# Four low weight parts made by ScalarE and an adding transfer, and a regrouped start, in a fused linear-attention and two-layer kernel

## The chip, the cores and the metric

One NeuronCore of a Trainium2 chip runs the whole program. The metric is device time in microseconds (us); the time before is the median of three runs. Engines are called PE (TensorE matmuls), PEld (its weight loads), DVE (VectorE), ACT (ScalarE), POOL (GpSimd) and SP (SyncE, which here issues nearly all transfers).

## The reference

The first stage is a linear attention with a complex decay: batch 4, 8 heads, 768 steps, head width 48. The two later stages are dense layers over 3072 tokens, with a width of 384 and a hidden width of 2048.

```
mag = sqrt(a_re*a_re + a_im*a_im)
scale = minimum(mag, 0.999) / (mag + 1e-06)
S_re, S_im = (a*scale) * (S_re + i S_im) + k v^T        (one step of 768)
y[t] = q[t] S_re
h = x @ w_in ;  x = (h - tanh(h)) @ w_out               (first layer)
h = x @ w_in ;  x = max(h, 0)**2 @ w_out                (second layer)
```

## The kernel before, in words

The 768 steps are cut into six chunks of 128, and with four batches this makes 24 units, numbered n = 4c + b for chunk c and batch b. Units 0 to 3 are chunk 0 and are computed ahead of everything else. Later units are spread over the steps of the first layer by a plan. The first layer works in blocks: one block is one slice m (128 of the 2048 hidden columns, m = 0 to 15) for 512 tokens. A block computes h with `g1`, then t, gh and gl (`act_parts`), and adds to three banks of `acc` with `g2`. Every factor is split into a rounded high part and a low part, so each product takes three matmuls: wh with xh, wh with xl, wl with xh.

The weights arrive as raw 64-bit words in a tile `st`, loaded by SP (`conv_load`, L205). `conv_do` (L214) rebuilds 32-bit floats in a tile `cv` with three DVE instructions (one TENSOR_SCALAR, two SCALAR_TENSOR_TENSOR). `cv` has two buffers, so slice m takes the buffer of slice m-2, and its first instruction has to wait until that buffer is no longer read. `conv_split` (L270) then calls `split_w` (L276): ACT rounds `cv` into `wh`, and DVE subtracts, `wl = cv - wh`. This happens for slices 0 to 15 of the first layer one after another, between 10 and 133 us.

The start is written out by hand in `START` (L32): a number and a name stand for one part of one unit (`0sq` is `a1` of unit 0, `0ln` is `a2`, `0ph` is `a3`, `0pc` is `a6l`), J is one third of a weight conversion. Between `<` and `>` the instructions of ACT and of DVE are chained, each engine issuing in the listed order; outside it a list scheduler orders each engine's queue at build time. For units 0 to 3, `a1` (L460) squares re and im into the two halves A and B of a tile `ab` (ACT for units 0 and 2, DVE for 1 and 3), and then one DVE instruction writes B = max(A, const) + B. `a2` (L472) is on ACT: logarithm of A in place, logarithm of B in place, X = exp(-B/2) into half G of a tile `fg`, exp(-A/2) in place. `a3` (L486) is on DVE: B = min(B, const) - X, then im = im * A. Half F of `fg` is first written later, in `a7` (L544). Two masks are made on DVE at L131 (`tri`) and L135 (`maskt`) from a mask that POOL writes at L112 to L122; these two are outside the chain. PE reads `maskt` first in the sums `pu`, and `tri` first from chunk 2 on.

After the first 160 us the rest of the first layer and the second layer follow, where the second layer's weights are converted on the way.

Of the kernel before, what the change touches and what calls it, by code (L numbers as in the profile page):

```python
# [12 lines left out]
F32 = mybir.dt.float32  # L13
# [3 lines left out]
AF = mybir.ActivationFunctionType  # L17
ALU = mybir.AluOpType
# [7 lines left out]
INV_2PI = 1.0 / (2.0 * math.pi)  # L26
# [3 lines left out]


START = """  # L32
0ld 3ld 1ld 2ld C W 0lq 3lq < T 0sq 0ln 3sq 3ln 0ph 0pc 1sq 1lq 1ln 3ph 3pc J J 2sq 2lq 2ln 1ph 1pc J
2ph 2pc 0lv 3lv 0ff 0ee 3ee 1ee 2ee g K > 0at 3at 1at 2at 0pu 0rd 1pu 3qe J 2lv 0qe 1rd 1sn 2pu
1qe 1kn 1qn 2qe 3pu 1lv J 0sn 1ff 0kn 0qn 0t0 1t0 0t1 1t1 0e1 0e0 1e0 3rd J J 0s1 0m1
2rd 3sn 2sn 1s0 1m0 1e1 0s0 2kn 3qn 3kn 0m0 3t0 1s1 2qn 3t1 2t0 0px 1m1 2e0 2t1 4ld 1px 1pU 0x 3e1
1x 0pU 2s0 2m0 0st 3e0 3s0 2e1 4sq J 4ln 1st 3s1 3pU 3m0 2s1 2m1 3st 3m1 2px 3px 2pU 2st B 2x 3x
"""
AHEAD = (1, 1, 1, 2, 2, 3, 4, 5, 5, 6, 7, 8, 8, 8, 9, 9, 10, 11, 11, 11, 12, 13, 13, 15, 15, 15, 16, 16)
JOINS = (4, 2, 3, 3, 4, 3, 2, 2, 2, 2, 3, 4, 3, 2, 2, 3, 4)  # L40


@with_exitstack
def kernel(
# [9 lines left out]
    nc = tc.nc  # L54
    B, S, HV, DP = v.shape
# [46 lines left out]
    def clear_strips():  # L102
        for z in strips:
            dve.memset(z, 0.0)
# [9 lines left out]
        out=maskab[:, 0], in_=maskab[:, 0], compare_op=ALU.is_ge, fill=0.0, base=0,  # L114
        pattern=[[1, P]], channel_multiplier=-1,
    )
    for g in range(4):
        m = maskab[32 * g:32 * g + 32, 1]
        nc.gpsimd.affine_select(
            out=m, in_=m, compare_op=ALU.is_ge, fill=0.0, base=-32 * (3 - g),  # L120
            pattern=[[1, P]], channel_multiplier=-1,
        )  # L122
    mask = maskab[:, 0]
# [3 lines left out]
        out=past, in_=past, compare_op=ALU.is_ge, fill=0.0, base=-1,  # L127
        pattern=[[-1, P]], channel_multiplier=1,
    )
    tri = const.tile([P, P], F32R, name="tri")  # L130
    nc.vector.tensor_copy(tri, mask)  # L131
    ones = const.tile([P, 1], F32, name="ones")
    nc.gpsimd.memset(ones, 1.0)
    maskt = const.tile([P, P], F32, name="maskt")
    nc.vector.tensor_scalar(maskt, mask, INV_2PI, None, op0=ALU.mult)  # L135
    b_tiny = const.tile([P, 1], F32, name="b_tiny")
    nc.gpsimd.memset(b_tiny, 1e-30)
    b_eps = const.tile([P, 1], F32, name="b_eps")
# [28 lines left out]
    ten, sp = (Turn(e) for e in (nc.tensor, nc.sync))  # L167
    dve = Turn(nc.vector, "dve")
    act_e = Turn(nc.scalar, "act")

    general = [False]
    act_set = {"name": None, "load": None, "ops": []}

    def table(*names):
        if act_set["name"] not in names and not general[0]:
            name = names[0]
            with ExitStack() as es:
                for o in act_set["ops"] or [act_set["load"]]:
                    if o is not None:
                        es.enter_context(tc.issue_after(o))  # L180
                load = act_e.preload_act_table_set(name).ins
            act_set.update(name=name, load=load, ops=[])

    def lut(*a, **kw):
        if general[0]:
            return act_e.activation(*a, **kw)
        with tc.issue_after(act_set["load"]):
            r = act_e.activation(*a, **kw)
        act_set["ops"].append(r.ins)
        return r  # L190
# [79 lines left out]
    def conv_split(layer, m, tf):  # L270
        wh = wpool.tile([P, n2], F32R, tag=f"wh{m}", name=f"wh{layer}_{m}")
        wl = wpool.tile([P, n2], F32R, tag=f"wl{m}", name=f"wl{layer}_{m}")
        split_w(wh, wl, tf)
        wts[layer, m] = (wh, wl)

    def split_w(wh, wl, tf):  # L276
        act_e.copy(wh, tf)
        dve.tensor_tensor(wl, tf, wh.bitcast(F32), op=ALU.subtract)
# [130 lines left out]
    def unit(n):  # L409
# [11 lines left out]
        V = {}  # L421
# [6 lines left out]
        def pair(name, *parts, pool=ap1, bufs=None):  # L428
            if early_unit:
                t = early(name)  # L430
            else:
                t = pool.tile([P, n2], F32, tag=name, name=f"{name}_{n}", bufs=bufs)
            V[name] = t
            V[parts[0]], V[parts[1]] = t[:, :HD], t[:, HD:]
            return t
# [36 lines left out]
        def a2():  # L472
            A, Bt = V["A"], V["B"]
            table("natural_log_exp_and_others")
            if c == 0:
                pair("fg", "F", "G")
            V["X"] = V["G"] if c == 0 else V["re"]
            if c == 0:
                lut(A, A, AF.Ln, bias=b_tiny)
                lut(Bt, Bt, AF.Ln)  # L480
            else:
                lut(V["ab"], V["ab"], AF.Ln, bias=b_tiny)
            lut(V["X"], Bt, AF.Exp, scale=-0.5, bias=b_eps)
            lut(A, A, AF.Exp, scale=-0.5)

        def a3():  # L486
            Bt, im = V["B"], V["im"]
# [343 lines left out]
        first = late == 0  # L831
# [22 lines left out]
    soon = {}  # L854
# [9 lines left out]
    def attn(s, low=0, high=10):  # L864
        for key, f in sorted(plan.get(s, []), key=lambda x: x[0]):
            if low <= key < high:
                f()
# [166 lines left out]
    def conv_upto(k):  # L1034
        while cdone[0] < k:
            conv_tick()
# [20 lines left out]
    s_first = 3 - (NST - 1)  # L1057
    pos = AHEAD
    assert len(pos) == NM - s_first
# [50 lines left out]
    def act_step(n, parts):  # L1110
        if n not in acts:
            acts[n] = act_parts(
                blocks[n][0], hs.pop(n), cur["pool"], lambda g: gs.__setitem__(n, g),
                third=NB0 <= n < NATT and n % 3 == 2, vector=NB0 - 1 <= n <= NB0,
            )
        for _ in range(parts):
            next(acts[n], None)

    def block_step(t):
        steps = [t - NB0 + NM]  # L1120
        chain["on"] = chain["dve"] = NB0 <= t < NATT
        chain["act"] = NB0 - 1 <= t < NATT
        if t < NB0:
            conv_upto(min(NM, blocks[t][2] + JOINS[t]))
            steps = ahead[t]
        visit = NB0 < t < NATT and (t - NB0) % 4 == 3
        if 0 < t <= NB and not visit:
            act_step(t - 1, 3)
        if t == NB0:
            share_banks()  # L1130
        if t < NB:
            l, g, m, cs = blocks[t]
            if t == NB0 - 1:
                h = ps_tile("h", "h")
                hs[t] = g1(l, m, xts[l, g], h, cs)
            for s in steps[:-1]:
                attn(s)
            if t == NB0 - 1:
                act_step(t, 1)
            if t == NB0 - 2:  # L1140
                conv_split(0, NM - 1, joined.pop(NM - 1))
            chain["act"] = NB0 - 2 <= t < NATT
            for s in steps[-1:]:
                attn(s, 0, 1.35)
                if visit:
                    act_step(t - 1, 1)
                attn(s, 1.35, 1.75)
                if visit:
                    act_step(t - 1, 1)
                attn(s, 1.75, 5)  # L1150
            if t != NB0 - 1:
                h = ps_tile("h" if t < NATT else "hxy"[t % 3], "h")[:, :cs.stop - cs.start]
                hs[t] = g1(l, m, xts[l, g], h, cs)
            for s in steps[-1:]:
                attn(s, 5, 6)
                if chain["on"]:
                    act_step(t, 1)
                if t == NB0:
                    clear_strips()
                attn(s, 6, 7)  # L1160
                if chain["on"] and (t - NB0) % 4 != 2:
                    act_step(t, 1)
                attn(s, 7, 10)
        if t == NATT:
            actx.close()
            cur["pool"] = fctx.enter_context(tc.tile_pool(name="ap3", bufs=3))
            cpool[0] = cur["pool"]
        if t == NB:
            finish()
            return  # L1170
        while cur["g2"] < NB and cur["g2"] <= t - (LAG if t >= NATT + 2 else 2):
            second_half(cur["g2"])
            cur["g2"] += 1
        if t == NATT + LAG:
            conv_ahead()
        if t >= NATT + LAG:
            for _ in range(2):
                if cdone[0] < len(cq):
                    conv_tick()
            m2 = cur["split"]  # L1180
            if m2 in joined and t >= NATT + LAG + m2:
                conv_split(1, m2, joined.pop(m2))
                cur["split"] += 1
        if t >= NATT + 2 * NM and t % 2 == 0 and cur["recheck"] < 2 * NM:
            conv_check(*divmod(cur["recheck"], NM))
            cur["recheck"] += 1
        if t >= NATT + 2 * NM and t % 4 == 1 and cur["signs"] < NU // 2:
            sign_check(cur["signs"])
            cur["signs"] += 1
        if t < NB and m == NM - 4:  # L1190
            if l == 1 and g < NG - 1:
                xts[1, g + 1] = get_x2(cur["pool"], x2g[g + 1])
            if l == 0 and g == NG - 1:
                xts[1, 0] = get_x2(cur["pool"], x2g[0])
# [1 line left out]


    first = {f"{n}{k}": f for n in range(B) for k, f in unit(n).items()}
    first.update(soon, C=clear_pads, W=conv_ahead, J=conv_tick, B=lambda: block_step(0))
    first.update({"<": lambda: chain.update(act=True, dve=True), ">": lambda: chain.update(act=False, dve=False),  # L1200
        "g": lambda: chain.update(gate=dve.last),
        "K": lambda: conv_split(0, 0, joined.pop(0))})
# [103 lines left out]
```

## Time and profile before

| | |
|---|---|
| median of three runs | 974.58 us (973.69 to 974.63) |
| the profiled execution's own time | 973.18 us |
| its span | 971.1 us |
| busy: PE, PEld | 950.1, 786.2 us |
| busy: ACT, DVE, POOL | 635.2, 540.7, 19.5 us |
| granted TensorE clock | 0.999 of full speed |

The span runs from the first to the last instruction that the profile shows; 2.1 us of the profiled execution's time lie around it. A matmul that is in flight counts as busy, so an engine shown as 98% busy may still be fed late. The start of a row is when an instruction began; a bracket behind it says how long the engine had been idle and what ended that.

### The profile page before, as it was taken

Reading aid. Unit: us, or ns where it says so; the run is one execution under the profiler, and the core shown is the slowest. Engines: PE = TensorE matmul, PEld = TensorE weight load, DVE = VectorE, ACT = ScalarE, POOL = GpSimd, SP = SyncE. Lnnn points to the kernel's source line nnn. Section 1 sums busy time; section 2 is a strip of 40 time slices with the busy share of each in tenths; the row PEclk is TensorE's granted clock in tenths of the full one; section 3 lists DMA queues with packets and bytes.
Section 4 is the critical chain, followed back from the end, with each engine's and each line's share of the span. In section 5 each row is a group of like instructions: output and inputs, shape, how many; then the busy total and the mean of one; then the engine's idle time right before and its main releaser. Section 6 shows DMA issues by size and latency. Waiting matters only on the chain.

```text
span 971.1 us, 18373 instructions
## 1 busy us (share of the span) xinstructions
PE 950.1 (98%) x7437; PEld 786.2 (81%) x7437; DVE 540.7 (56%) x902; ACT 635.2 (65%) x1110; POOL 19.5 (2%) x43
## 2 busy tenths in 40 slices
PE   5999999999999999999999999999999999999997
PEld 2888788888888888888888888888888888888886
DVE  7999987666666666665548993132322322322111
ACT  8879978777777777786534455465666665555442
POOL 2000000000000000000000010000000000000000
PEclk9999999999999999999999999999999999999999
DMA  8345413222322232221136552063444353330001
GB/s 315 131 148 165 151 45 92 59 58 64 101 68 70 63 92 64 69 75 42 58 126 224 176 169 79 1 195 104 163 143 140 93 176 113 130 97 31 33 1 34
DMA packets 53481, 100.99 MB, mean 104 GB/s; under 512 B 19712, under 2 KB 29200, under 8 KB 53392
## 3 DMA queue, kind: packets, MB, share of 16 engines
q1 hardware_dynamic: 53248, 99.65, 32.4%
q8 instruction: 59, 0.97, 0.4%
q14 instruction: 30, 0.25, 0.1%
q10 hardware_dynamic: 144, 0.13, 0.0%
HBM read 87.08 MB, written 9.46 MB: 99 GB/s over the span
## 4 chain that ended last, share of the span: by engine, by line
PE 89%; ACT 5%; DVE 5%; DMA 1%; issue 1%; ACTq 0%
PE h L161 39%; PE acc L161 38%; PE px L161 3%; PE strips L161 2%; PE pk L161 1%; PE pq L161 1%; ACT ab L161 1%; PE pU L161 1%; DVE cv L161 1%; ACT L161 1%; PE pu L161 1%; PE sc L161 1%; PE pc L161 1%; ACT fg L161 1%; ACT ee L161 1%
## 5 line engine op out<-in xcount | busy, mean ns | idle before, releaser
L161 DVE TENSOR_TENSOR gl<-t,gh 128x512 fp32r<-128x512 f32 (+1 forms) x193 | 132.2, 685 | 215.4 <-ACT gh L161 215.1
L161 ACT ACTIVATE t<-h 128x512 f32<-128x512 f32 (+1 forms) x193 | 114.6, 594 | 194.0 <-PE h L161 191.4
L161 PE MATMUL acc<-gh,wh 128*128 128x512 f32 (+1 forms) x579 | 229.3, 396 | 0.0
L161 PE MATMUL h<-xh,wh 128*128 128x512 f32 (+1 forms) x579 | 228.0, 394 | 0.6 <-DVE t L161 0.4
L161 PE MATMUL h<-xh,wl 128*128 128x512 f32 (+1 forms) x579 | 225.1, 389 | 0.0
L161 PE MATMUL acc<-gl,wh 128*128 128x512 f32 (+1 forms) x579 | 225.0, 389 | 0.0
L161 PE MATMUL acc<-gh,wl 128*128 128x512 f32 (+1 forms) x579 | 224.8, 388 | 0.0
L161 PE MATMUL h<-xl,wh 128*128 128x512 f32 (+1 forms) x579 | 224.0, 390 | 0.0
L161 ACT CAST gh<-t 128x512 fp32r<-128x512 f32 (+1 forms) x191 | 118.0, 618 | 87.0 <-PE acc L161 46.2
L161 PEld LDWEIGHTS h<-xh,wh 128*128 128x128 f32 x579 | 108.7, 188 | 26.6 <-issue 3.2
L161 PEld LDWEIGHTS h<-xh,wl 128*128 128x128 f32 x579 | 108.7, 188 | 22.7
L161 PEld LDWEIGHTS acc<-gh,wl 128*128 128x128 f32 x579 | 108.7, 188 | 22.6
L161 PEld LDWEIGHTS acc<-gl,wh 128*128 128x128 f32 x579 | 108.9, 188 | 21.9 <-DVE gl L161 0.2
L161 PEld LDWEIGHTS acc<-gh,wh 128*128 128x128 f32 x579 | 108.8, 188 | 21.6
L161 PEld LDWEIGHTS h<-xl,wh 128*128 128x128 f32 x579 | 108.7, 188 | 21.1
L161 DVE TENSOR_TENSOR t<-h,t 128x512 f32<-128x512 f32 (+1 forms) x97 | 65.8, 679 | 59.8 <-ACT t L161 59.7
L161 ACT ACT_TABLE_LOAD x63 | 80.8, 1283 | 1.7 <-PEq L1288 0.8
L161 ACT ACTIVATE t<-t 128x512 f32<-128x512 f32 x96 | 60.3, 628 | 1.6
L161 DVE TENSOR_TENSOR wmin<-wmin,cz 128x768 bf16<-128x768 bf16 x32 | 17.8, 557 | 57.4 <-ACT cz L161 57.4
L161 DVE TENSOR_TENSOR wm<-strips,maskab 128x512 f32<-128x512 f32 x32 | 21.8, 690 | 29.1 <-PE strips L161 29.1
L161 DVE SCALAR_TENSOR_TENSOR jw<-st,jw 128x768 int32<-128x768 int32 x32 | 30.4, 950 | 0.2
L161 DVE SCALAR_TENSOR_TENSOR cv<-st,cv 128x768 int32<-128x768 int32 x32 | 30.4, 949 | 0.2
(141 smaller groups left out, 977.7 us busy)
## 6 DMA issues: line engine op xcount, KB each, us to landing
st<-in_w_dram SPq DMA_DIRECT2D x32, 768.0 KB
sr<-in_w_dram SPq DMA_DIRECT2D x32, 768.0 KB
ri<-in_ri_dram SPq DMA_DIRECT2D x24, 384.0 KB
qk<-in_qk_dram SPq DMA_DIRECT2D x24, 384.0 KB
vz<-in_v_dram SPq DMA_DIRECT2D x16, 384.0 KB
x2d<-x2t SPq DMA_DIRECT2D x18, 256.0 KB
xf<-x2d SPq DMA_DIRECT2D x6, 768.0 KB
ss<-in_ri_dram SPq DMA_DIRECT2D x12, 384.0 KB
```

Source lines behind the costliest of these rows:

```text
L161: r = op(*a, **kw)
```

## The change

The DVE subtraction of `conv_split` is replaced for slices 4, 5, 6 and 14 of the first layer: ACT rounds `cv` into `wh` as before, then writes `wl = -wh`, and a transfer issued from the POOL queue adds `cv` to `wl`. In chunk 0, the logarithm and the exponential of A go to half F of `fg` instead of in place. The two masks move behind a new letter M, which stands in `START` right behind the letters `<` and `T`, so that they are the first two DVE instructions of the chain.

```diff
-0ld 3ld 1ld 2ld C W 0lq 3lq < T 0sq 0ln 3sq 3ln 0ph 0pc 1sq 1lq 1ln 3ph 3pc J J 2sq 2lq 2ln 1ph 1pc J
+0ld 3ld 1ld 2ld C W 0lq 3lq < T M 0sq 0ln 3sq 3ln 0ph 0pc 1sq 1lq 1ln 3ph 3pc J J 2sq 2lq 2ln 1ph 1pc J
...
+BY_DMA = (4, 5, 6, 14)
...
-    nc.vector.tensor_copy(tri, mask)
...
-    nc.vector.tensor_scalar(maskt, mask, INV_2PI, None, op0=ALU.mult)
...
+    def more_masks():
+        dve.tensor_copy(tri, mask)
+        dve.tensor_scalar(maskt, mask, INV_2PI, None, op0=ALU.mult)
...
-        split_w(wh, wl, tf)
+        if layer == 0 and m in BY_DMA:
+            act_e.copy(wh, tf)
+            act_e.mul(wl, wh.bitcast(F32), -1.0)
+            nc.gpsimd.dma_start(out=wl, in_=tf, accum_op=ALU.add)
+        else:
+            split_w(wh, wl, tf)
...
             if c == 0:
-                lut(A, A, AF.Ln, bias=b_tiny)
+                V["A"] = V["F"]
+                lut(V["A"], A, AF.Ln, bias=b_tiny)
                 lut(Bt, Bt, AF.Ln)
...
-            lut(A, A, AF.Exp, scale=-0.5)
+            lut(V["A"], V["A"], AF.Exp, scale=-0.5)
```

## Rows read from the trace of the kernel before

**Rows 1.** The page: busy tenths of POOL in 40 slices of the span.
```profile
POOL 2000000000000000000000010000000000000000
```

**Rows 2.** Waits of PE by engine and line, 51 us to the end.
```profile
PE pk L161 <- DVE kn L161: 1.0, 2, 0.7
PE px L161 <- issue: 0.6, 2, 0.3
PE h L161 <- DVE t L161: 0.4, 2, 0.2
PE h L161 <- ACT xh L161: 0.3, 1, 0.3
```

**Rows 3.** Windows of 4 us: busy PE, PEld, DVE, ACT, POOL, PEclk, DMA share, GB/s.
```profile
16.00:20.00 4.00, 4.00 (x9) 2.85 (x9) 4.00 (x7) 3.98 (x9) 0.00 (x0) 1.00 1.04 404
...
56.00:60.00 4.00, 4.00 (x26) 3.48 (x25) 4.00 (x8) 2.39 (x5) 0.00 (x0) 1.00 0.20 81
60.00:64.00 4.00, 4.00 (x22) 3.35 (x21) 3.97 (x6) 3.97 (x7) 0.00 (x0) 1.00 0.54 197
```

**Rows 4.** Timeline of the first 16 us: ACT, DVE and POOL at chunk 0.
```profile
1.79 1.29 POOL L119 TENSOR_SCALAR_AFFINE_SELECT maskab<-maskab 32x128 f32<-32x128 f32 x4
...
4.92 0.56 DVE L161 SCALAR_TENSOR_TENSOR ab<-ab 128x384 f32<-128x384 f32 x1 [4.92 <-ACT ab L161]
...
5.59 0.61 ACT L161 ACTIVATE ab<-ab,b_tiny 128x384 f32<-128x384 f32 x1 [0.70 <-POOL state L397]
6.11 0.51 ACT L161 ACTIVATE ab<-ab 128x384 f32<-128x384 f32 x1
...
6.88 0.22 DVE L131 CAST tri<-maskab 128x128 fp32r<-128x128 f32 x1
...
7.35 0.56 DVE L161 SCALAR_TENSOR_TENSOR ab<-ab,fg 128x384 f32<-128x384 f32 x1
...
9.88 0.62 ACT L161 ACTIVATE ab<-ab,b_tiny 128x384 f32<-128x384 f32 x1 [0.17 <-DVE ab L161]
...
12.74 0.56 DVE L161 SCALAR_TENSOR_TENSOR ab<-ab 128x384 f32<-128x384 f32 x1 [0.49 <-ACT ab L161]
...
13.34 0.61 ACT L161 ACTIVATE ab<-ab,b_tiny 128x384 f32<-128x384 f32 x1 [0.64 <-DVE ab L161]
```

**Rows 5.** Tile cv: DVE's subtractions (ns min/median/max, first and last start).
```profile
L161 DVE TENSOR_TENSOR wl<-cv,wh x16: 937/948/958, 19.9 to 131.9; 128x768 fp32r<-128x768 f32 x16
```

**Rows 6.** Timeline of slices 4 to 6 on ACT, DVE, SP and PE.
```profile
48.76 0.83 ACT L161 CAST wh<-cv 128x768 fp32r<-128x768 f32 x1 [1.28 <-DVE cv L161]
...
53.58 0.55 DVE L161 TENSOR_SCALAR cv<-st 128x768 int32<-128x768 int32 x1
...
55.67 0.42 DVE L161 TENSOR_TENSOR gl<-t,gh 128x256 fp32r<-128x256 f32 x1
...
56.14 0.39 PE L161 MATMUL acc<-gl,wh 128*128 128x256 f32 x1
...
64.90 0.39 PE L161 MATMUL h<-xh,wl 128*128 128x512 f32 x1
...
48.75 10.69 SPq L161 DMA_DIRECT2D st<-in_w_dram  x3
```

**Rows 7.** A transfer of 384 KB: issue on SP and the DVE instruction that waited for it; chain: a 768 KB load.
```profile
133.78 0.35 SPq L161 DMA_DIRECT2D qk<-in_qk_dram  x1
...
136.88 0.96 DVE L161 TENSOR_TENSOR qk<-qk,ee 128x768 f32<-128x768 f32 x1 [0.79 <-DMA qk<-in_qk_dram]
...
102.89 5.39 DMA st<-in_w_dram
```

**Rows 8.** Slice 14: ACT's rounding and PE's first use of its low part; PE's longest wait.
```profile
123.27 0.84 ACT L161 CAST wh<-cv 128x768 fp32r<-128x768 f32 x1
...
132.12 0.40 PE L161 MATMUL h<-xh,wl 128*128 128x512 f32 x1
...
133.90 0.61 PE L161 MATMUL pk<-ident,kn 128*96 128x128 f32 x4 [0.69 <-DVE kn L161]
```

More of the change, by code (lines that the diff above doesn't have):

```diff
@@ L1198 @@
     first = {f"{n}{k}": f for n in range(B) for k, f in unit(n).items()}
-    first.update(soon, C=clear_pads, W=conv_ahead, J=conv_tick, B=lambda: block_step(0))
+    first.update(soon, C=clear_pads, M=more_masks, W=conv_ahead, J=conv_tick, B=lambda: block_step(0))
     first.update({"<": lambda: chain.update(act=True, dve=True), ">": lambda: chain.update(act=False, dve=False),
```

## The prediction, made before the changed kernel ran

> **What bounds the kernel now.** I read the waits of PE first. From 51 us, where the first layer begins, to the end, PE waits 1.0 + 0.6 + 0.4 + 0.3 = 2.3 us in all [rows 2]. So for 920 us the order of matmuls is the limit, and a change can win there at most those 2.3 us. Of them 1.4 us end on DVE (pk and h); the two others are no affair of this change. What is left to win lies before 51 us, where PE follows a chain of ACT and DVE: whatever makes that chain shorter moves everything behind it. The windows come next. In the eleven windows from 16 to 60 us (the first and the last in [rows 3]) DVE is busy for 3.84 to 4.00 of 4 us, so DVE sets the pace from 16 us on; ACT is idle 1.6 us of 56 to 60, and full (3.97 of 4) from 60 to 64 [rows 3]. The timeline of the first 16 us shows where DVE still waits: 0.49 us before 12.74, for ACT [rows 4].
>
> **The logarithm of chunk 0 into another tile.** In place, the logarithm of A must wait until DVE has read A. Unit 0: DVE's instruction runs from 4.92 to 5.48, and ACT, which is 0.70 us idle, begins the logarithm at 5.59 [rows 4]. Written elsewhere, it begins 0.70 us earlier, beside DVE's instruction; the logarithm of B then takes the place at 5.59. Before, it began at 6.11 [rows 4], so all that ACT does later in unit 0 comes 0.52 earlier. Unit 1 also waits, 0.17 at 9.88 [rows 4]; with the overlap between neighbours on ACT (the 0.61 from 5.59 reach past 6.11, 0.09) that is 0.26, as its square is then long done. Together 0.78: ACT's square of unit 2, and DVE's instruction that waits for it at 12.74, come at 11.96. At 13.34 ACT waits 0.64 once more [rows 4], which it also loses, so ACT gains some 1.3, but from there DVE is the one that sets the pace.
>
> **The masks.** They cost DVE 0.22 us each (`tri` at 6.88, `maskt` right behind it), ahead of the instruction at 7.35 [rows 4]. Its input from ACT is there 0.52 earlier, so with the masks still in between it would begin about 7.25, and without them when DVE is free at 6.88: 0.47 of the 0.78 need the masks to be gone. The new place costs nothing: POOL has written the whole mask at 1.79 + 1.29 = 3.08, and DVE does nothing before 4.92 [rows 4]. That idle time is the cover; if POOL were 2 us later, both masks would stand ahead of the first square's sum.
>
> So DVE is 0.78 us earlier at 12. It has hardly any idle time from there to 51, so this arrives whole at the first block unless an input comes too late. The transfers are the candidate: the engines are full until 20 us (DMA share 1.04, 404 GB/s [rows 3]). The ends are 0, if DVE then waits for loads, and 1.3, if ACT's gain counts. I take 0.78, since the loads of qk stand ahead of v's in SP's queue and are needed one by one.
>
> **Four subtractions less on DVE.** One takes 0.948 us [rows 5]. Three of them (slices 4, 5, 6) follow roundings of which the first begins at 48.76 [rows 6], the fourth (slice 14) follows the one at 123.27 [rows 8]. That is 4 x 0.95 = 3.8 us of DVE, but PE sees it only where it waits for DVE, 1.4 us after 51 [rows 2]. The largest, 0.69 at 133.90 [rows 8], is for `kn`, which stands in DVE's queue behind slice 15's subtraction, and that one waits for ACT; there slice 14's 0.95 us helps only if the build orders the queues anew. Ends: 0 and 1.4. I take half, 0.7, as the longest wait has a removed subtraction in the 11 us before it.
>
> **Four more instructions on ACT.** The negated copy is not in the trace; its nearest row is the rounding with the same shape and types, 0.83 us [rows 6]. Slice 4's fits: ACT was idle 1.28 us just ahead of it [rows 6]. Slice 5's comes soon after, and up to 60 us ACT has 1.6 us free in four [rows 3]. Slice 6's comes at about 60, where ACT is full, and makes later tanh work late by up to 0.83; I take 0, because ACT's idle time before it is mostly waiting for DVE, which is now earlier. The ends are 0 and 0.83.
>
> **Four adding transfers.** They go through POOL's queue, where nothing stands from the first slices until the middle of the span [rows 1], so nobody queues behind them there; SP's queue is not touched. Each moves 384 KB from `cv` to `wl`. The lower bound is a load of that size: issued at 133.78, waited for at 136.88, 3.1 us [rows 7]. An addition also reads its destination, so the bytes read are those of the 768 KB load in the chain, 5.39 us [rows 7]; I take that as nearest. Both ends may add: at 48.75 SP begins three such weight loads [rows 6], and behind one the upper end is 3.1 + 5.39 = 8.5 us. Now who waits. PE reads slice 4's low part first at 64.90 [rows 6], some 14 us after it is issued, so that is hidden. Slice 14 has less: rounding from 123.27, the negation until some 124.8, use at 132.12 [rows 8], 7.3 us. And a new wait appears on DVE: `cv` has two buffers, and slice 6 may not overwrite slice 4's before the transfer has read it. Slice 6 begins at 53.58 [rows 6]; slice 4's negation ends at about 50.3, so 5.4 us end at 55.7. Behind DVE's waiting instruction stands the gl at 55.67, which PE took at 56.14 [rows 6], almost at once. In the old order DVE would do it 1.1 us late (55.7 + 0.5 + 0.6 against 55.67, where 0.95 is already won by the missing subtraction). The build orders DVE's queue anew with that wait in it, and other work is there, so I put 0 in the sum, and 1.1 in the range.
>
> The Trainium skill, "DMA: Bandwidth & Descriptors", section "Anatomy of one DMA — SWDGE (gpsimd) path", fits a plain transfer from that queue by 2.0 us plus bytes over 436 GB/s. By it these 393,216 bytes would be an estimated 2.9 us, and the 1.1 would vanish; no row here shows that path.
>
> **The sum.** 973.18 of the profiled execution, less 0.78, less 0.7: 971.7. That execution was 1.4 us below the median of 974.58, so the median comes out at 974.58 - 1.48 = 973.1. What a measurement of this kernel can tell from no change is about 0.2%, 1.95 us; the forecast is inside it.
>
> **Rivals.**
> - *All of it arrives* (0.33). ACT's 1.3 counts, because the chain from 16 to 51 goes through ACT too, and all 2.3 us of waiting close as the queues are ordered anew: 974.58 - 3.6 = 971.0 at the far end, some 971.9 in the middle. For it: DVE and ACT are both near full, so relief spreads. Against it: 0.9 of the waits do not end on DVE.
> - *ACT gives it back* (0.09). Slice 6's negation delays tanh by 0.83 in the full windows [rows 3]: 974.58 - 0.78 + 0.83 = 974.6.
> - *The logarithm does not move* (0.06). The profile names POOL for the wait at 5.59, not DVE [rows 4]. If POOL's memsets held it, unit 0's 0.52 is lost: 973.6. Against it: the two later waits name DVE.
> - *The transfer is slow* (0.14), and the kernel slower. Place: DVE's first instruction of slice 6. Price: 1.1 us at 5.39, and one us for each further us, so at 8.5 us 4.2 on DVE and, through gl, on PE: 974.58 - 0.78 + 4.2 = 978.0. It decides from about 7.0 us per transfer, where the loss passes 0.78 + 1.95; there slice 14's 7.3 us run out as well. For it: DVE, which is in order, has no slack at gl.
>
> The Trainium skill, "SBUF — State Buffer", section "SBUF: two separate sides", says that GpSimd cannot write such a transfer's descriptors while VectorE runs an instruction in a mode that takes the port pair both share. By that rule each of DVE's TENSOR_SCALARs (0.55 us [rows 6]) would hold a transfer back for its own length, and the price of the last rival would grow by that much per transfer. No row here shows it.
>
> **How the numbers follow.** The forecast itself has 0.38. Faster by over 0.2%: 0.33. Within 0.2%: 0.38 + 0.09 + 0.06 = 0.53. Slower by over 0.2%: 0.14. The range goes down to 971.2, past the middle of the first rival and nearly to its end, and up to 976.4: 973.1 with neither 0.7 (+0.7), with the 1.1 and the 0.83, and a transfer 0.7 us longer than taken. It leaves out some 0.1 above and less below. The forecast's own range, with the start and half the waits within their nearer ends, is 972.6 to 974.1.
>
> **What would show it.** In the first 16 us the logarithm of B at 5.59 instead of 6.11, the masks before 4.92, and DVE's instruction at 12.74 at about 11.96. The first matmul of h some 0.8 us earlier. No fewer than 12 subtractions `wl`, four ACT instructions of about 0.83, four POOL issues. PE's waits on DVE after 51 us below 1.4. The forecast is wrong if h begins no earlier, if PE's waits after 51 grow, or if DVE shows a wait of over 2 us ahead of a TENSOR_SCALAR on `cv`.

## The result, and the profile after

The changed kernel takes 983.39 us (median of 6 runs, 982.48 to 986.07) beside 973.75 for the kernel before: a ratio of 1.0100, interval 1.0087 to 1.0113. It is 9.6 us slower where 973.1 (971.2 to 976.4) was forecast. The profiled execution took 983.37 with a span of 981.6, so it stands for the median; before it was 973.18 and 971.1.

To tell body from end, every run below is read by two numbers: when DVE's last output instruction (`ot<-strips,part`, the last compute instruction of the program) begins, and how much of the span follows it.

```profile
965.58 0.42 DVE L161 TENSOR_TENSOR ot<-strips,part 128x256 f32<-128x256 f32 x1 [1.46 <-PE strips L161]
```
```profile
974.14 0.42 DVE L160 TENSOR_TENSOR ot<-strips,part 128x256 f32<-128x256 f32 x1 [1.46 <-PE strips L160]
```

The first is before, the second after. 974.14 - 965.58 = 8.56 us of the loss lie ahead of that instruction. Behind it the span goes on for 981.6 - 974.14 = 7.5 us, where it was 971.1 - 965.58 = 5.5: another 1.9.

The first 16 us went as forecast. Timeline of DVE and ACT after, which answers to [rows 4]:

```profile
1.88 0.29 DVE L160 CAST tri<-maskab 128x128 fp32r<-128x128 f32 x1 [1.88 <-POOL maskab L114]
2.09 0.21 DVE L160 TENSOR_SCALAR maskt<-maskab 128x128 f32<-128x128 f32 x1
...
4.90 0.61 ACT L160 ACTIVATE fg<-ab,b_tiny 128x384 f32<-128x384 f32 x1
5.43 0.52 ACT L160 ACTIVATE ab<-ab 128x384 f32<-128x384 f32 x1
...
11.80 0.56 DVE L160 SCALAR_TENSOR_TENSOR ab<-ab 128x384 f32<-128x384 f32 x1
...
50.33 0.39 PE L160 MATMUL h<-xh,wh 128*128 128x256 f32 x1
```

The masks stand in DVE's idle time, B's logarithm begins at 5.43 (5.59 forecast), the instruction once at 12.74 begins at 11.80 (11.96 forecast), and the first matmul of h at 50.33 instead of 51.05.

The loss is in the next 30 us. The waits of PE from 51 us, which answer to [rows 2], grew from 2.3 to 7.9 us:

```profile
PE h L160 <- DVE t L160: 4.5, 3, 4.0
PE pk L160 <- DVE kn L160: 1.9, 3, 0.7
PE px L160 <- issue: 0.6, 2, 0.3
PE acc L160 <- DVE gl L160: 0.6, 1, 0.6
PE h L160 <- ACT xh L160: 0.3, 1, 0.3
```

The long one (4.0 us), and what led to it, is read in the timeline of ACT, POOL, DVE and PE from 49 to 76 us (it answers to [rows 6]; rows of one engine and moment are picked, in order of time):

```profile
49.58 0.83 ACT L160 CAST wh<-cv 128x768 fp32r<-128x768 f32 x1 [2.64 <-DVE cv L160]
...
51.62 0.84 ACT L160 ACTIVATE wl<-wh 128x768 fp32r<-128x768 f32 x1
...
52.78 1.00 POOL L279 DMA_DIRECT2D wl<-cv  x1 [46.30 <-ACT t L160]
54.22 0.42 DVE L160 TENSOR_TENSOR gl<-t,gh 128x256 fp32r<-128x256 f32 x1
55.04 0.42 DVE L160 TENSOR_TENSOR t<-h,t 128x256 f32<-128x256 f32 x1 [0.40 <-ACT t L160]
59.05 0.56 DVE L160 TENSOR_SCALAR cv<-st 128x768 int32<-128x768 int32 x1 [3.58 <-DMA wl<-cv]
59.53 0.42 DVE L160 TENSOR_TENSOR gl<-t,gh 128x256 fp32r<-128x256 f32 x1
...
60.01 0.39 PE L160 MATMUL acc<-gl,wh 128*128 128x256 f32 x1 [0.59 <-DVE gl L160]
...
61.51 0.63 ACT L160 CAST gh<-t 128x512 fp32r<-128x512 f32 x1 [4.72 <-DVE t L160]
...
69.06 0.56 DVE L160 TENSOR_SCALAR cv<-st 128x768 int32<-128x768 int32 x1 [0.98 <-DMA wl<-cv]
...
70.87 0.60 ACT L160 ACTIVATE t<-h 128x512 f32<-128x512 f32 x1
...
73.20 0.68 DVE L160 TENSOR_TENSOR t<-h,t 128x512 f32<-128x512 f32 x1
...
73.94 0.80 PE L160 MATMUL h<-xh,wh 128*128 128x512 f32 x1 [4.01 <-DVE t L160]
```

Slice 6 may not overwrite slice 4's `cv` before the transfer has read it. DVE stands 3.58 us at that instruction (59.05), with a `gl` right behind it. It is not the `gl` of 55.67 in [rows 6]: that one, for the first half of the block, now stands at 54.22, ahead of the wait. The one at 59.53 is for the second half, and before it stood here:

```profile
57.20 0.42 DVE L161 TENSOR_TENSOR gl<-t,gh 128x256 fp32r<-128x256 f32 x1
```

PE itself waits only 0.59 for that `gl`, because it has other matmuls. But ACT, which takes what DVE makes, then stands 4.72 us. From 61.5 it has its whole work of the stretch still to do, and a tanh (`t<-h`) comes at 70.87, 3.93 later than before (66.94). DVE's `t<-h,t` that takes it comes at 73.20, 5.06 later than before (68.14). DVE still has two slice steps in its queue ahead of it, and these are late by a second wait of the same kind: 0.98 at 69.06, where slice 8 waits for slice 6's transfer. From there to 73.20 DVE is never idle, so that wait arrives whole. PE, out of other work, has waited 4.01 us at 73.94. A short wait for PE at one place became a long one 14 us later: the idle time had gone to ACT. The windows after show it engine by engine, the second and third line answering to [rows 3] (columns as there):

```profile
52.00:56.00 4.00, 3.95 (x21) 2.96 (x21) 2.52 (x7) 3.88 (x8) 1.00 (x1) 1.00 0.86 283
56.00:60.00 4.00, 3.41 (x20) 2.76 (x18) 0.95 (x3) 0.63 (x2) 0.86 (x1) 1.00 1.00 197
60.00:64.00 4.00, 3.73 (x19) 3.10 (x20) 3.97 (x6) 2.31 (x4) 0.00 (x0) 1.00 0.20 48
64.00:68.00 4.00, 4.00 (x20) 3.30 (x19) 3.40 (x5) 3.97 (x7) 0.84 (x1) 1.00 0.93 243
68.00:72.00 4.00, 1.94 (x9) 1.28 (x7) 2.98 (x6) 3.97 (x7) 0.00 (x0) 1.00 0.58 207
72.00:76.00 4.00, 2.06 (x4) 1.51 (x5) 4.00 (x7) 2.33 (x4) 0.00 (x0) 0.59 0.12 1
76.00:80.00 4.00, 4.00 (x11) 2.87 (x9) 1.57 (x3) 1.11 (x3) 0.00 (x0) 0.56 0.46 123
```

DVE falls from 4.00 to 0.95 of 4 us in 56 to 60; ACT is the full one in 64 to 72; PE is idle in 70 to 74. In the last two lines the granted clock is 0.59 and 0.56: after its idle 4 us PE works a while at the lower of its two levels (1.2 of 2.4 GHz), with 4.00 us busy and 11 matmuls where the windows around have some 20. The block whose first matmul stood at 68.88 begins at 73.94, 5.06 late; the next, once at 74.41, begins at 82.10, 7.69 late. So 2.63 us are lost after the wait is over, with the clock low. At the last output instruction the distance is 8.56.

### The profile page after: what moved, and what is told of

Its sections match the earlier page's. It is cut to its first block, busy times and chain, and to the rows that moved or that the text cites. A ratio compares the mean times of both kernels' runs of the same rounds, so it can differ in the third digit from the quotient of the medians.

```text
span 981.6 us, 18391 instructions
## 1 busy us (share of the span) xinstructions
PE 953.3 (97%) x7437; PEld 788.6 (80%) x7437; DVE 538.5 (55%) x898; ACT 638.1 (65%) x1114; POOL 23.0 (2%) x47
## 4 chain that ended last, share of the span: by engine, by line
PE 85%; DVE 2%; ACT 2%; DMA 1%; issue 0%; SPq 0%; ACTq 0%; DVEq 0%
PE h L160 38%; PE acc L160 37%; PE px L160 3%; PE strips L160 2%; PE pk L160 1%; PE pq L160 1%; PE pU L160 1%; PE pu L160 1%; PE pc L160 1%; ACT L160 1%; PE sc L160 0%; ACT ab L160 0%; DVE cv L160 0%; DVE kn L160 0%; ACT fg L160 0%
## 5 line engine op out<-in xcount | busy, mean ns | idle before, releaser
L160 DVE TENSOR_TENSOR t<-h,t 128x512 f32<-128x512 f32 (+1 forms) x97 | 65.9, 680 | 61.5 <-ACT t L160 61.4
```

What stands on the lines that cost most here:

```text
L160: r = op(*a, **kw)
```

## The experiments

A trace can show where the time went, not how much of it each part of the change would cost alone. Theory W says VectorE's wait for the adding transfers; A, ScalarE's four added instructions; S, the start's new order. In the table, "body" is the begin of the last output instruction against 965.58, "end" the span behind it, both of one profiled execution; the median is that of all runs.

| run | body | end | median | ratio (interval) |
|---|---|---|---|---|
| the change | +8.6 | 7.5 | 983.39 | 1.0100 (1.0087 to 1.0113) |
| start_only | +1.3 | 5.6 | 974.66 | 1.0009 (0.9999 to 1.0018) |
| neg_only | +0.8 | 5.5 | 974.88 | 1.0007 (0.9998 to 1.0016) |
| dma_only | +5.4 | 7.7 | 980.42 | 1.0064 (1.0049 to 1.0080) |
| own_cv | +3.5 | 7.9 | 978.47 | 1.0042 (1.0028 to 1.0055) |
| small | +3.9 | 7.5 | 978.73 | 1.0055 (1.0039 to 1.0070) |
| own_small | +0.3 | 7.6 | 976.44 | 1.0030 (1.0017 to 1.0043) |
| plain | +3.3 | 7.6 | 979.63 | 1.0067 (1.0052 to 1.0083) |
| only14 | +1.5 | 7.2 | 976.65 | 1.0028 (1.0017 to 1.0040) |
| tiny | +0.2 | 5.6 | 973.39 | 0.9999 (0.9990 to 1.0008) |
| tiny_read | +0.9 | 5.6 | 973.90 | 1.0000 (0.9991 to 1.0009) |
| tiny4 | +1.7 | 8.3 | 976.99 | 1.0036 (1.0022 to 1.0049) |
| start_x | +0.5 | 5.5 | 973.79 | 1.0002 (0.9993 to 1.0011) |
| pool_sub | +8.3 | 5.7 | 979.53 | 1.0057 (1.0043 to 1.0071) |

One execution differs from the median of its kernel by up to 1.5 us (2.1 in pool_sub), so a body below 1.5 says no more than "about as before".

**start_only.** The start's edits alone, no transfer.

```diff
-BY_DMA = (4, 5, 6, 14)
+BY_DMA = ()
```


> The change with no slice made by a transfer: only the logarithm's new tile and the two masks first. Theory W (the loss is VectorE waiting for the adding transfers): 0.7 us under the kernel before, some 973.1 against 973.8, first matmul of h at about 50.3 us, no stretch with a lowered granted clock. Theory A (the loss is ScalarE's four added instructions): the same 973.1. Theory S (the loss comes from the new order of the start): over 980.

974.66 beside 974.04: no difference that can be told, and none of the 0.7 us expected. The gain did reach PE: the first h stands at 50.27, 0.78 before 51.05. It is gone within three us. Timeline of DVE in this run:

```profile
50.80 0.56 DVE L160 TENSOR_TENSOR xl<-px,xh 128x384 fp32r<-128x384 f32 x1
51.27 0.95 DVE L160 TENSOR_TENSOR wl<-cv,wh 128x768 fp32r<-128x768 f32 x1
52.14 0.55 DVE L160 TENSOR_TENSOR xl<-px,xh 128x384 fp32r<-128x384 f32 x1
```

The build has put slice 4's subtraction between the two that give `xl`. The matmul that needs the second stands at 52.74, where before it stood at 52.69. On ACT the gain was gone already: its second pass of `xh`, from which that `xl` is made, begins no earlier than before. It stands behind the rounding of slice 4 (49.45 here, 48.76 before) and a copy of `state`. First before, then this run:

```profile
50.76 0.48 ACT L161 ACTIVATE xh<-px 128x384 fp32r<-128x384 f32 x1
```
```profile
51.03 0.49 ACT L160 ACTIVATE xh<-px 128x384 fp32r<-128x384 f32 x1
```

**neg_only.** The four slices by ScalarE's negation, the transfers left out.

```diff
-            nc.gpsimd.dma_start(out=wl, in_=tf, accum_op=ALU.add)
```


> The whole change without the four adding transfers (the low parts of slices 4, 5, 6 and 14 are left at minus their high parts, so the addition is left out). ScalarE's negations stay and VectorE's four subtractions are gone. Theory W: some 973, no waits on a transfer. Theory A: some 983, with ScalarE late from 60 us. Theory S: some 983.

974.88, against start_only's 974.66 (some 973 was expected). So A falls: with four more instructions on ACT (0.83 to 0.84 us each) the loss is not there. The run gives the net of the exchange, four subtractions less on DVE against four negations more on ACT, and the net is zero; a small gain on the one side paid back on the other is not excluded. PE's waits from 51 us are 3.1 us in both runs, of which those on DVE fall from 1.6 to 1.4 and those on ACT grow from 0.3 to 0.9. What the transfers could have won at best is therefore about zero here.

**own_cv.** Slices 4, 5 and 6 are rebuilt in buffers of their own (tiles whose weights come later), so that no later slice waits for a transfer.

```diff
-            t = spool.tile([P, n2], I32, tag="cv", name=f"cv{layer}_{m}", bufs=2)
+            own = {4: "wl15", 5: "wl11", 6: "wh15"}.get(m)
+            if own:
+                t = wpool.tile([P, n2], F32, tag=own, name=f"cv{layer}_{m}").bitcast(I32)
+            else:
+                t = spool.tile([P, n2], I32, tag="cv", name=f"cv{layer}_{m}", bufs=2)
```


> The whole change, but the rebuilt words of slices 4, 5 and 6 lie in buffers of their own (places of low parts 15 and 11 and of high part 15 that are free then), so that no conversion has to wait until a transfer has read its source. Transfers and negations stay. Theory W: no wait of VectorE on the transfer, no lowered clock, 972.4 to 973.2. Theory A: as slow as the whole change, some 983. Theory S: some 983.

978.47 beside 974.04, where 972.4 to 973.2 was expected: of 9.6 us 4.4 remain, 2.4 of them in the end. So W has a little over half of it, and something else the rest. The waits of DVE from 50 to 85 us in this run, and its timeline:

```profile
DVE cv L160 <- DMA st<-in_w_dram: 3.4, 2, 1.8
```
```profile
63.47 0.56 DVE L160 TENSOR_SCALAR cv<-st 128x768 int32<-128x768 int32 x1 [1.81 <-DMA st<-in_w_dram]
```

DVE waits for the staged weight loads now, which it did not in this stretch before. The load waited for here was issued at 57.5; neg_only issues it at 57.7, and DVE takes it at 61.89 without a wait (it waits 0.7 for a load once, at 76). The window of 56 to 60 us shows why, own_cv first, then neg_only (the last two columns are DMA share and GB/s):

```profile
56.00:60.00 4.00, 4.00 (x27) 3.63 (x26) 3.97 (x7) 3.11 (x5) 0.95 (x2) 1.00 1.08 215
```
```profile
56.00:60.00 4.00, 4.00 (x27) 3.59 (x26) 3.97 (x7) 3.07 (x6) 0.00 (x0) 1.00 0.36 104
```

The DMA engines are full, and move only 215 GB/s, though they moved 404 at a share of 1.04 where they carried loads alone [rows 3]. The queues of own_cv from 52 to 64 us (packets, MB, share of 16 engines):

```profile
q0 software_dynamic: 406, 1.13, 50.2%
q1 hardware_dynamic: 382, 2.05, 49.5%
```

The adding transfers take as much engine time for 1.13 MB as the loads for 2.05.

**dma_only.** The transfers alone, with the start as before.

> The four low parts by negation and transfer, with the start as before (logarithm in place, masks outside the chain). Theory W: the kernel before plus 10.3, some 984, with the wait of over 3 us ahead of slice 6 and the lowered clock after it. Theory A: 984 too, but without that wait. Theory S: 974 to 975.

980.42, not the 984 expected: the transfers alone cost 6.4 us, two thirds of the loss, so S falls (with start_only) and W stands. In this run DVE waits on the same buffers 3.3 us in all, the longest 2.4 instead of 3.58. The lowered clock came as expected, 0.63 from 72 to 76 us, after PE had waited 2.11 us. With the start's edits the whole change is some 3 us worse, though they cost nothing by themselves. Each kernel's queues are ordered anew, so how much a wait costs may depend on what the build has put next to it; no run holds the order fixed to show that.

**small.** The wait stays, the bytes go: an eighth of each transfer.

```diff
-            nc.gpsimd.dma_start(out=wl, in_=tf, accum_op=ALU.add)
+            nc.gpsimd.dma_start(out=wl[:, :96], in_=tf[:, :96], accum_op=ALU.add)
```


> The changed kernel with each of the four transfers cut to the first 96 of 768 columns, so that the waits, the queue and ScalarE's instructions stay and an eighth of the bytes is moved (the low parts of the other columns are left as the negated high parts: part of the computation is left out). Theory W by size (the landing of 4 to 6 us is the data's own time, which also holds up the staged loads): landing under 3 us, VectorE's waits on the buffers under 1 us together, no clock loss, median 976.8 (975.5 to 978), 2 us of it the end. Rival (the landing is a fixed cost of the software queue): landing still over 3.5 us, VectorE waits over 2 us, 981 or more.

The median landing (from a transfer's issue until its data have arrived) falls from 4.6 to 2.3 us as forecast, but the first transfer still takes 4.1, DVE waits 1.5 for a buffer instead of under 1, and the time is 978.73, over the range. The rival of a fixed landing of 3.5 or more falls. The size is half of the cost; of the 5.1 us that remain 2 are the end, and whether the short wait makes the rest the next run tells.

**own_small.** Both together: own buffers and an eighth of the bytes.

> Both at once: slices 4, 5, 6 rebuilt in buffers of their own, as in the run where the wait is taken away, and each transfer cut to 96 of 768 columns (the low parts of the other columns stay the negated high parts: part of the computation is left out). Theory WB (what the transfers cost ahead of the program's end is two things: VectorE's wait for the buffer, and the staged loads that the transfers' bytes hold up, on the DMA engines): neither is left, so the last output tile comes within 1.5 us of before's 965.6 (as without any transfer, 966.4), median 976.5 (975.5 to 977.5), 2 us of it the longer end. Rival (the four issues on GpSimd's queue or the build's other order cost by themselves): last output tile at 968.5 or later, median 978.5 or more.

976.44 where 976.5 was expected, and the body within 0.3 us of before. The clock stays high (1.00 in each window from 52 to 100 us). With neither wait nor bytes nothing of the 8.6 us is left, so the four issues on POOL (0.84 to 1.00 us each) and this run's order cost nothing. Either remedy alone leaves 3.5 to 3.9. The two causes can't be added up, since fewer bytes also shorten the wait: in small 1.5 us of it are left.

**plain.** The same transfers as copies, without adding.

```diff
-            nc.gpsimd.dma_start(out=wl, in_=tf, accum_op=ALU.add)
+            nc.gpsimd.dma_start(out=wl.bitcast(F32), in_=tf)
```


> The changed kernel with its four transfers as plain copies, not adding (the low parts then come out as copies of the whole: part of the computation is left out). Theory WB with adding as the dear part: landing median under 3.6 us instead of 4.6, VectorE's longest wait on a buffer under 2.6 us instead of 3.6, the same longer end, 979.5 (977.5 to 981.5). Rival (a copy between two tiles costs the same, adding is free): landing 4.3 to 4.9, wait 3.3 to 3.9, 983 (981.5 to 985).

979.63, as expected; the longest wait on a buffer is 2.7, where under 2.6 was expected. The landing (min, median, max), first of the changed kernel, then of plain:

```profile
DMA to landing us min/median/max: 3.9/4.6/6.3
```
```profile
DMA to landing us min/median/max: 2.6/3.0/5.3
```

The queue's share of the DMA engines from 52 to 64 us falls from 34.4% to 15.8% for the same 0.79 MB. The adding costs 1.6 us a transfer and more than doubles the engine time. In both kernels, and in small, the longest is slice 4's, about 2 us over the median: a 768 KB weight load is issued just ahead of it, at 52.4 or 52.5.

**only14.** Slice 14 alone by a transfer.

> The changed kernel with slice 14 alone by a transfer; slices 4, 5, 6 by VectorE's subtraction as before. Theory W (the cost is VectorE's wait in the stretch from 50 to 80 us, where staging and splits are dense) with Q: no wait of VectorE on a transfer over 1 us, granted clock 1.0 throughout, median 976.6 (975.5 to 977.6), of which 2 us lie in the program's end. Rival (every such transfer costs its share, a quarter of the 9.6 us): over 2.2 us of body beside the end, 979 or more.

976.65 (976.6 expected): no wait of DVE on a buffer, the clock high (1.00 in each window from 52 to 160 us), and of 3.0 us some 1.7 in the longer end. The fourth transfer, away from the dense stretch, costs little by itself.

**tiny and tiny_read.** The kernel before with one 512 B transfer on POOL's queue, unread and read.

```diff
+    spare = const.tile([P, 1], F32, name="spare")
+    nc.gpsimd.dma_start(out=spare, in_=b_tiny)
```


> The kernel before with one GpSimd transfer of 512 B (a constant of 128 values to a spare tile) near its start, that nobody waits for. Theory Q (a program that uses the software queue ends later): body as before, the stretch from the last output tile's VectorE instruction to the end of the span 7.5 to 7.9 us instead of 5.5, as in every kernel with such transfers so far; median 976.0 (975.4 to 976.8). Rival (the longer end comes of the size or of the adding of the transfers): 974.0 (973.6 to 974.5), end of 5.5 us.

> The kernel before with one GpSimd transfer of 512 B, of a constant that the late sign passes read as their bias, so that now somebody waits for a software transfer. Theory E1 (the end is longer when an engine waits on that queue's semaphore): 7 us or more between the last output tile and the end of the span, 975.7 (975 to 976.5). Rival E2 (the end is longer for another reason, such as the amount of the queue's descriptors or code): 5.5 us, 973.6 (973.1 to 974.4).

(The read one copies `b_re`, and the sign passes take `spare` as bias.) Both have the end as before, 5.6 us, and the time of before. Theory Q and its successor E1 fall: using the queue, or waiting for it, is not what lengthens the end.

**tiny4.** Four such transfers, unread.

> The kernel before with four GpSimd transfers of 512 B near its start, that nobody waits for. Theory E3 (the longer end goes by the number of transfers on that queue: SyncE ends the program by a list of waits, one more for each, 12 rows of them with four full transfers and 10 without): 7.2 us or more between the last output tile and the end of the span, a stall of 1.5 us or more between two of SyncE's last waits, 975.6 (974.9 to 976.4). Rival E4 (the longer end comes of the bytes or packets that the queue has moved, or of when): 5.4 to 5.7 us, 973.7 (973 to 974.4).

976.99 and an end of 8.3 us, although 2 KB were moved. E4, bytes or packets, falls. The program's end is a list of waits on SP; its rows in the kernel before, in tiny, in tiny4 and after the change (count, duration in ns, first and last start):

```profile
L1241 SPq EVENT_SEMAPHORE  x8: 17/17/17, 969.2 to 969.7; - x8
```
```profile
L1243 SPq EVENT_SEMAPHORE  x8: 17/17/17, 969.3 to 969.9; - x8
```
```profile
L1244 SPq EVENT_SEMAPHORE  x8: 17/17/17, 971.2 to 973.5; - x8
```
```profile
L1250 SPq EVENT_SEMAPHORE  x8: 17/17/17, 977.7 to 980.0; - x8
```

Eight instructions that follow each other within 0.6 us take 2.3 in the last two. So four transfers are enough for the longer end, whatever they move. In only14, with one transfer and an end of 7.2, SP stops too, but behind these eight: they end at 971.2 and its next list begins at 972.8 (969.7 and 969.8 in the kernel before). That next list has 10 rows without a transfer, 11 with one and 12 with four, so it does not grow by one for each, as E3 had it. Why SP stops, and why it does so in only14 and not in tiny, is not shown. The kernels with a long end show one or two more packets on the instruction queue (31 or 32 against 30), but start_only has 31 and a short end.

The time of tiny4 lies 0.6 over its range because of the start. Its issues take POOL 2.29 us ahead of the clearing of `state`, and that now falls from 6.81 to 8.75 us, on DVE's two masks. They take 1.89 and 1.82 us instead of 0.22 each [rows 4], and h begins at 52.49 instead of 51.05:

```profile
6.94 1.89 DVE L131 CAST tri<-maskab 128x128 fp32r<-128x128 f32 x1
```

**start_x.** The start's edits, with slice work held behind both xl.

```diff
+            with ExitStack() as es:
+                if (layer, m) == (0, 4):
+                    es.enter_context(tc.issue_after(chain["xl"]))
+                split_w(wh, wl, tf)
```
(and the same around slice 5's last bit step.)

> The start's edits alone (no transfers, VectorE subtracts all low parts), and slice 4's subtraction and slice 5's last bit step made to stand behind both subtractions that give xl. Theory X (the start's 0.78 us reaches PE's first h at 50.3 but dies at the second xl, because the build puts a 0.95 us slice instruction between the two): second xl over by 51.9 instead of 52.69, blocks 2 to 5 start 0.7 earlier than before instead of 0.2, median 973.5 (972.9 to 974.1). Rival (the gain is absorbed later whatever the order, by PE's waits on kn and px): blocks 2 to 5 early, later blocks not, 974.4 (974 to 975).

973.79: as before, so theory X falls in its size. The second xl now begins at 51.83 instead of 52.14 (51.9 expected), no earlier, since it waits for PE; the third block begins 0.27 before the old time instead of 0.13. The rest of the 0.78 is held by the chain from px through ACT to xl itself: ACT's second pass of xh begins at 51.21 here. Where the last 0.27 goes the runs do not show.

**pool_sub.** GpSimd subtracts, with no negation and no transfer.

```diff
-            act_e.mul(wl, wh.bitcast(F32), -1.0)
-            nc.gpsimd.dma_start(out=wl, in_=tf, accum_op=ALU.add)
+            nc.gpsimd.tensor_tensor(wl, tf, wh.bitcast(F32), op=ALU.subtract)
```


> The changed kernel with GpSimd subtracting the low parts of the four slices instead of ScalarE's negation and the transfer. GpSimd's nearest row is xh's pass of 128x512 at 799 ns; with two operands and 768 columns I take 1.2 to 2.5 us each. Theory WB: no transfer, no wait over 1 us on a buffer if a subtraction ends within 2 us, the end as before: 974.3 (973.4 to 975.5), as with the negations alone, since VectorE's four subtractions were no bound there. Rival 1 (relief of VectorE is worth 0.7 us once nothing is given back): 973.0 or less. Rival 2 (VectorE's own instructions slow down beside GpSimd's): VectorE's rows in the stretch longer by 10% or more, 976 or more.

979.53, where 974.3 was expected: rival 2. The profiled execution took 981.63, so its body may stand some 2 us too high. Timeline of POOL and DVE in this run:

```profile
50.72 2.20 POOL L278 TENSOR_TENSOR wl<-cv,wh 128x768 fp32r<-128x768 f32 x1 [44.25 <-PE pU L160]
51.62 2.12 DVE L160 SCALAR_TENSOR_TENSOR cv<-st,cv 128x768 int32<-128x768 int32 x1
54.68 1.85 POOL L278 TENSOR_TENSOR wl<-cv,wh 128x768 fp32r<-128x768 f32 x1 [1.76 <-ACT wh L160]
55.12 1.83 DVE L160 TENSOR_SCALAR cv<-st 128x768 int32<-128x768 int32 x1 [0.58 <-DMA st<-in_w_dram]
61.12 1.85 POOL L278 TENSOR_TENSOR wl<-cv,wh 128x768 fp32r<-128x768 f32 x1 [4.59 <-PE h L160]
61.27 2.52 DVE L160 SCALAR_TENSOR_TENSOR cv<-st,cv 128x768 int32<-128x768 int32 x1
```

DVE's steps of 0.95 and 0.55 us take 2.12, 1.83 and 2.52. Each ends 0.4 to 0.8 us after POOL's instruction does (52.92, 56.53, 62.97), as if it began its work only then. POOL takes 2.0 us for what DVE does in 0.95, and DVE stands still meanwhile. The Trainium skill, "SBUF — State Buffer", section "Who interferes with whom", says that GpSimd and some of VectorE's instructions share a pair of ports, and that whoever holds it blocks the other for its whole instruction; the three rows agree.

No version beats the kernel before.

## Why the prediction was wrong

**Right: the start, up to PE.** Logarithm, masks, 11.80, and 0.72 earlier at the first h (0.78 forecast), so the rival "the logarithm does not move" falls. **Wrong: that it stays.** "This arrives whole at the first block" was true and not enough. The step looked for a limit between 12 and 51 us; the limit was at 52, at the second xl. In start_only it stands behind a slice's subtraction on DVE, in a window that the prediction's own reading calls full of DVE work; with that moved away (start_x), PE and ACT's pass of xh still hold it. start_only gives 0 (974.66 beside 974.04), not 0.78.

**Wrong: the 0.7 for four subtractions.** PE's waits on DVE did not shrink below the 1.4 us of before (1.6 in start_only, 1.4 in neg_only), and neg_only beside start_only is 0. With the start and the waits both worth nothing, "all of it arrives" falls too.

**Right, as a net: ACT's negations at 0.** neg_only stands 0.2 us over start_only, not 0.83, so "ACT gives it back" does not make the loss.

**The step that failed: "The build orders DVE's queue anew with that wait in it, and other work is there, so I put 0 in the sum".** The sum's 0 for the transfers, and the range's 1.1, measured 8.6 us ahead of the last output instruction. The place was named, DVE's first instruction of slice 6, and only half of what stands behind it: the gl of 55.67 went ahead of the wait, and the build put the wait directly ahead of the next gl, with no other work between. And the buffer came free at 59.05, not 55.7. Of these 3.35 us, 2.48 are that the transfer starts at 52.78 where the negation was taken to end at 50.3: the rounding comes 0.82 later than in [rows 6], ACT has two passes of xh and one of state between it and the negation (51.62), and POOL issues 0.3 after that ends. 0.87 are the transfer itself, 6.27 against 5.4. The sum counted the length of the transfer and took its start for granted. Two of the forecast's own signs of being wrong came: PE's waits after 51 us grew, and DVE shows a wait of over 2 us ahead of a TENSOR_SCALAR on `cv`.

**What the rival had, and what it lacked.** "The transfer is slow" was the case that came, at 6.3 us, below the 7.0 from which it was said to decide. Its price rule, one us of PE for each us of DVE, is refuted: for DVE's 3.58 PE lost 0.59 at gl, and 4.01 some fourteen us later, when ACT had to make up for 4.72 idle us and DVE had waited 0.98 more for slice 6's transfer, and 2.63 more at the lower clock. That the transfers' bytes hold up the weight loads, 3.5 us of body with the wait removed (own_cv), was not in any case; the prediction saw that a load could delay the transfer, not the reverse. Nor was the end, 1.9 us.

**The rules that were weighed.** By the Trainium skill, "DMA: Bandwidth & Descriptors", section "Anatomy of one DMA — SWDGE (gpsimd) path", a plain transfer of this size is an estimated 2.9 us; plain's median of 3.0 agrees. The fit does not describe the adding transfer, at a median of 4.6. That DVE's instructions hold back the writing of descriptors is shown by no run: the issues of the adding transfers take 0.84 to 1.01 us throughout.

**Of the 10.5 us between the spans of the two profiled executions**, then: 8.6 from the wait and the bytes together (own_small without both: 0.3), and 1.9 from the longer end that four transfers bring. ACT's instructions and the start cost about nothing by themselves; why the transfers cost 3 us more with the new start than without it (dma_only) stays open.

## What to carry to other kernels

When work is moved off an engine to a transfer, find first which buffer the transfer keeps busy, and follow the wait on it to the instructions queued behind: here DVE's queue handed it on, and it came out longer, at another engine, 14 us later. Count when the transfer starts, instruction by instruction on its producer, and not only how long it takes; and look at what else the DMA engines carry then. Before any of it, take the instructions away without the replacement: neg_only would have shown that there was nothing to win.

## What the runs showed of the hardware that was not expected

- An adding transfer of 384 KB between two tiles lands in 4.6 us (median), a plain one in 3.0, and takes 2.2 times the engine time (34.4% against 15.8% of 16 engines over 12 us).
- Four transfers on GpSimd's queue lengthen the program's end by 1.9 to 2.7 us even at 512 B each and unread (tiny4: 8.3 against 5.5); one small one does not, while one of full size did (only14: 7.2).
- A DVE instruction that meets a subtraction of GpSimd's takes 1.83 to 2.52 us instead of 0.55 to 0.95 (pool_sub); two that meet GpSimd's clearing of `state` take 1.82 and 1.89 instead of 0.22 (tiny4).
- After 4.0 us without a matmul PE's granted clock was 0.59 and 0.56 in the next two windows of 4 us, and 1.00 from 80 us on. In dma_only it was 0.63 in one window after a wait of 2.11; in plain, after one of 2.95, it was 1.00 in each window from 52 to 100 us. What decides it these runs do not show.
